# Values of a batch in one tile, keys and queries in one transfer, and tails that leave their list later: attention with two feed-forward layers on one core

## The chip, the cores and the metric

The kernel runs on one NeuronCore of a Trainium2 chip. The metric is the device time of one execution in microseconds (us). Before the change it is 997.43 us, the median of three runs (996.99 to 999.98).

The engines are named as the profile names them: PE is TensorE (matmuls), PEld its weight loads, DVE is VectorE, ACT is ScalarE, POOL is GpSimd, SP is SyncE, whose queue issues nearly all DMAs; a few go out from ACT's queue. PE writes to PSUM, here eight banks of 128 x 512 floats.

## The reference

Four batches, eight heads, 576 positions, head size 64. The attention has a causal mask and a bias from running sums; its output goes through two feed-forward layers.

```python
scores = scale * np.matmul(q, k.transpose(0, 1, 3, 2))
cum = np.cumsum(np.maximum(s, 0.0), axis=-1)
bias = -(cum[:, :, :, None] - cum[:, :, None, :])
scores = np.where(causal, -1000000000.0, scores + np.minimum(bias, 0.0))
attn = softmax(scores)                     # over the keys
x = np.matmul(attn, v)                     # (4, 8, 576, 64), then 2304 tokens x 512
x = ((x @ w_a) * (x @ w_b)) @ w_out        # 512 -> 1536 -> 512
h = x @ w_in                               # 512 -> 2048
out = (np.maximum(h, 0.0) + alpha * np.minimum(h, 0.0)) @ w_out2
```

## The kernel before, in words

**Blocks.** The 2304 tokens are worked off in four feed-forward blocks. Blocks 0, 1 and 2 hold the first 512 positions of batches 0, 1 and 2; block 3 holds those of batch 3 and, besides, the last 64 positions of all four batches, 768 tokens in all. Only block 3 uses a scheme with fewer products (`ffn_seven`). A feed-forward product is made of three matmuls, high part by high part, low by high and high by low (`mm3`, lines 1199 to 1201; the last layer's are lines 1847 to 1849); one of them is 128x512. A block has 816 of them.

**Attention.** `first_attention` does batch 0 before any feed-forward. The attention of batch b + 1 runs inside feed-forward block b, as a list of steps (`attention`): `s01` and `s23` make the scores of a pair of heads, `av` (matmuls at line 810, for batch 0 at line 817) multiplies probabilities by values.

**Tails.** The last 64 queries of every head are the tails. There is one unit for each batch and pair of heads, sixteen in all, in a list of their own (`all_tails`) with three steps each: `ready` loads what the unit needs and makes its bias, `s4` (line 750) computes the scores, `av_b` (line 837) multiplies by the values. Between `s4` and `av_b` lies a chain: reductions on DVE, exponentials on ACT, scaling, a transposition on DVE into `zt`, a DMA from `zt` to DRAM (`zd`), and one back into `pb`, of which there is one buffer. The order of units is that of batches 0, 1, 2, 3. `TAILS = 0.7, 2.85` says over which part of the blocks' time the list is spread.

**The planner.** The class `Order` holds a clock of its own (`run.now`) that adds up planned times of PE and of every chain of steps. It decides in which order and on which engine instructions are recorded; on the chip each engine follows its own list strictly, and semaphores do the rest. A step of the tails leaves the list (`tail_due`) when its share of the time is reached and `possible` says that the planner's clock has what the step needs: `seen` asks for data that are there at most 100 ns from now.

**Values.** `load_v(b, hp, u)` loads the values of one pair of heads, once for `av` (u = 0) and once more for the tails (u = 1), into one of four buffers `vb`. For batch 0 and u = 0 that is one DMA. Otherwise it is four DMAs of 64 KB, one for each fourth partition, and for the tails two more of 16 KB after a `memset` on POOL (line 474).

**Keys and queries.** `load_kq(b, hp, 0)` loads a pair's keys and queries for batches 0 and 1 with two DMAs of 256 KB, one for each half of the partitions. In DRAM (`kq_a`) every head has its rows twice.

**DMA issue.** All DMAs of SP and ACT share eight semaphores in rotation (DMAHW0 to 7 in the order below); a DMA waits for the former user of its semaphore to have landed.

Of the kernel before, what the change touches and what calls it, by code (L numbers as in the profile page):

```python
# [65 lines left out]
TAILS = 0.7, 2.85  # L66
# [151 lines left out]
def attention_two_moe_kernel(  # L218
# [37 lines left out]
    W32, RAW, KQ, VB, CB, KL, TOPS = 4, 5, 3, 4, 3, 2, 2  # L256
# [4 lines left out]
    of_raw, of_kq, of_w32, of_w, of_vb, of_t, of_pb, of_c0, of_c1, of_kl = (  # L261
        Slots(n) for n in (RAW, KQ, W32, 6, VB, 4, 1, CB, 2, 0)
# [195 lines left out]
    def load_v(b, hp, u):  # L458
        c0 = 2 * hp * D
        got = []  # L460

        def chain():
            yield of_vb
            vr = raw.tile([P, 5, 2 * D], F32, name="vb", tag="vb", bufs=VB)
            got.append(vr)
            if b + u < TURN:
                yield from dma(
                    vr[:, 0:4, :], v[b, 0:QA, c0:c0 + 2 * D].rearrange("(c p) d -> p c d", p=P)
                )
                return  # L470
            keys = v[b, 0:QA, c0:c0 + 2 * D].rearrange("(c j k) d -> j k c d", j=4, k=32)
            if u:
                yield {"pool": 240}, SEEN
                nc.gpsimd.memset(vr[:, 4, :], 0.0)
            for j in range(4):
                yield from dma(vr[j::4, 0:4, :], keys[j])
                if u and j < 2:
                    k0 = QA + 32 * j
                    yield from dma(vr[j::4, 4, :], v[b, k0:k0 + 32, c0:c0 + 2 * D])

        v_t[b, hp, u] = got, run.spawn(chain(), slack=SL_QK)
# [44 lines left out]
    def load_sums(b, h, u):  # L526

        got = []

        def chain():  # L530
            yield of_c1 if u else of_c0
            nk = S if u else QA
            cb = raw.tile([P, nk], F32, name=f"cb{u}", tag=f"cb{u}", bufs=2 if u else CB)
# [260 lines left out]

    def av(b, hp):
# [6 lines left out]
        got, ready = v_t.pop((b, hp, 0))  # L802
        run.need(ready)
        at = slot()
        pv = banks[at]
        for r in range(4 if turned else 0):
            for c in range(r + 1):
                for j in range(2):
                    p = pts[(2 * hp + j) % 4].rearrange("p (i t n) -> p i t n", i=4, n=32)
                    nc.tensor.matmul(  # L810
                        pv[64 * j:64 * j + 64, r * P:(r + 1) * P],
                        got[0][:, c, j * D:(j + 1) * D], p[:, :, r * (r + 1) // 2 + c, :],
                        start=c == 0, stop=c == r,
                    )
        for c in range(0 if turned else 4):
            for j in range(2):
                nc.tensor.matmul(
                    pv[64 * j:64 * j + 64, c * P:QA], got[0][:, c, j * D:(j + 1) * D],
# [3 lines left out]
        run.give(of_vb)  # L822
# [3 lines left out]
    def av_b(b, hp):  # L826

        settle((b, hp, 4))
        got, ready = v_t.pop((b, hp, 1))
        run.need(ready)  # L830
# [3 lines left out]
        for c in range(5):  # L834
            for j in range(2):
                p = pb.rearrange("p (i t n) -> p i t n", i=4, n=32)
                nc.tensor.matmul(  # L837
                    pv[64 * j:64 * j + 64], got[0][:, c, j * D:(j + 1) * D],
# [3 lines left out]
        run.give(of_vb)  # L842
# [6 lines left out]
    def first_attention():  # L849
# [16 lines left out]
        for i in range(HP):  # L866
            load_v(0, i, 0)
# [48 lines left out]
    def attention(a):  # L916
# [7 lines left out]
        def loads(i):  # L924
            load_kq(a, i, 0)
            if a >= SUMS_PE:
                for j in range(2):
                    load_sums(a, 2 * i + j, 0)
            load_v(a, i, 0)
# [16 lines left out]
    def all_tails():  # L946

        def ready(b, i):
            load_kq(b, i, 1)
            load_sums(b, i, 1)  # L950
            load_v(b, i, 1)
            biases(b, i, (4,))

        units = [(b, i) for b in range(B) for i in range(HP)]
# [254 lines left out]
    def seen(*chains):  # L1209
        return all(c.done and c.time <= run.now + 100 for c in chains)  # L1210

    def possible(f, args):
# [6 lines left out]
        if f == av:  # L1219
            keys = [(b, 2 * hp + k, r) for k in range(2) for r in (0, 2, 3)]  # L1220
            return all(k in e_t and seen(e_t[k]) for k in keys) and seen(v_t[b, hp, 0][1])
# [728 lines left out]
```

## Time and profile before

| | us |
|---|---|
| runs without a profile, median (range) | 997.43 (996.99 to 999.98) |
| the profiled execution | 1002.63 |
| its span on the core | 1000.8 |
| PE busy in the span | 971.4 |
| DVE, ACT, POOL busy | 752.6, 551.9, 222.4 |

The profiled execution is longer than its span by what lies ahead of the first instruction and behind the last. PE is the engine that is nearly always busy. A share of busy time over the whole span hides where it pauses, so the stretches of the blocks and the pauses themselves are shown further down. A time in brackets behind an instruction is the idle time of its engine just before it, with what ended it; "issue" there means that the profile shows nothing that the engine waited for. PEclk is the clock that the chip granted to PE, as a share of 2.4 GHz.

### The profile page before, as it was taken

What the parts mean: (1) busy time and instruction counts of PE and PEld (TensorE: products, weight loads), DVE (VectorE), ACT (ScalarE), POOL (GpSimd) and SP (SyncE); (2) the same over time, 40 slices, a digit from 0 to 9 for tenths busy, and PEclk for the clock granted to TensorE, in tenths of its full rate; (3) what the DMA queues carried; (4) which work ended last, traced back from release to release, by engine and by line L of the source; (5) the groups of instructions that cost most, each with busy time, mean ns of one, the idle gap of its engine ahead of it and who ended that gap; (6) DMA issues with size and microseconds to landing.
All of it is one profiled execution on the core that took longest, in us unless ns stands there. A gap on an engine that the chain in (4) does not pass through costs nothing.

```text
span 1000.8 us, 15919 instructions
## 1 busy us (share of the span) xinstructions
PE 971.4 (97%) x5267; PEld 815.3 (81%) x5267; DVE 752.6 (75%) x1735; ACT 551.9 (55%) x1156; POOL 222.4 (22%) x287
## 2 busy tenths in 40 slices
PE   7999999999979997999999999999999999999997
PEld 6677877788868875778888887888899999999996
DVE  8897779868767874978568577877587888787782
ACT  7866666667554534665356354554463334476453
POOL 3131111112243342543124444342000000000000
PEclk9999999999998998999999999999999999999999
DMA  9599987799787888589578849666213222112202
GB/s 261 156 317 357 334 287 263 280 323 326 256 262 234 261 239 265 157 272 300 179 240 245 269 136 278 207 183 215 84 43 100 70 84 75 53 49 79 64 1 63
DMA packets 140115, 196.78 MB, mean 197 GB/s; under 512 B 35776, under 2 KB 79808, under 8 KB 140032
## 3 DMA queue, kind: packets, MB, share of 16 engines
q1 hardware_dynamic: 130240, 177.93, 56.8%
q10 hardware_dynamic: 9792, 17.83, 4.7%
q8 instruction: 41, 0.67, 0.3%
q14 instruction: 42, 0.34, 0.1%
HBM read 152.13 MB, written 43.59 MB: 196 GB/s over the span
## 4 chain that ended last, share of the span: by engine, by line
PE 83%; DVE 7%; DMA 6%; issue 2%; ACT 1%; SPq 0%; POOL 0%; ACTq 0%; DVEq 0%; POOLq 0%
PE bank L1199 19%; PE bank L1200 18%; PE bank L1201 18%; PE bank L1847 4%; PE bank L1849 4%; PE bank L1848 4%; PE bank L810 3%; PE bank L1700 2%; PE bank L1699 2%; PE bank L1701 2%; DMA zd<-zt 2%; DVE z L298 2%; PE bank L552 1%; PE bank L750 1%; PE bank L837 1%
## 5 line engine op out<-in xcount | busy, mean ns | idle before, releaser
L1199 PE MATMUL bank<-xh,wh 128*128 128x512 f32 (+1 forms) x620 | 239.7, 387 | 1.9 <-DVE g L298 1.9
L1200 PE MATMUL bank<-xl,wh 128*128 128x512 f32 (+1 forms) x620 | 235.0, 379 | 1.1 <-DVE xl L298 1.1
L1201 PE MATMUL bank<-xh,wl 128*128 128x512 f32 (+1 forms) x620 | 234.6, 378 | 0.0
L290 ACT ACTIVATE wh<-raw 128x512 fp32r<-128x512 f32 (+1 forms) x198 | 116.0, 594 | 155.0 <-PE bank L1200 74.6
L1199 PEld LDWEIGHTS bank<-xh,wh 128*128 128x128 f32 x620 | 116.7, 188 | 26.0 <-issue 3.2
L1200 PEld LDWEIGHTS bank<-xl,wh 128*128 128x128 f32 x620 | 116.9, 188 | 20.0 <-DVE xl L298 1.8
L1201 PEld LDWEIGHTS bank<-xh,wl 128*128 128x128 f32 x620 | 116.8, 188 | 19.5
L307 DVE TENSOR_TENSOR wl<-raw,wh 128x512 fp32r<-128x512 f32 (+1 forms) x140 | 88.5, 646 | 46.8 <-ACT wh L290 46.0
L307 POOL TENSOR_TENSOR wl<-raw,wh 128x512 fp32r<-128x512 f32 x64 | 85.8, 1342 | 105.3 <-ACT wh L290 69.2
L282 ACT ACTIVATE z<-z,mn 128x512 f32<-128x512 f32 (+4 forms) x144 | 82.7, 577 | 18.6 <-DVE mn L298 18.0
L1199 PE MATMUL bank<-gh,wh 128*128 128x512 f32 (+1 forms) x240 | 91.4, 381 | 1.6 <-ACT gh L290 1.6
L1200 PE MATMUL bank<-gl,wh 128*128 128x512 f32 (+1 forms) x240 | 90.0, 375 | 0.2 <-DVE gl L307 0.2
L1201 PE MATMUL bank<-gh,wl 128*128 128x512 f32 (+1 forms) x240 | 89.6, 373 | 0.0
L980 ACT ACTIVATE top<-raw 128x512 f16<-128x512 bf16 x90 | 69.2, 783 | 17.5 <-DMA raw<-in_w_dram 16.7
L1847 PE MATMUL bank<-wh,gh 128*128 128x512 f32 x192 | 76.5, 399 | 0.0
L1849 PE MATMUL bank<-wh,gl 128*128 128x512 f32 x192 | 74.9, 390 | 0.0
L1848 PE MATMUL bank<-wl,gh 128*128 128x512 f32 x192 | 74.8, 390 | 0.0
L290 ACT ACTIVATE gh<-g 128x512 fp32r<-128x512 f32 x84 | 52.4, 624 | 36.6 <-DVE g L298 35.4
L307 DVE TENSOR_TENSOR gl<-g,gh 128x512 fp32r<-128x512 f32 x70 | 55.6, 794 | 19.0 <-ACT gh L290 18.0
L625 POOL TENSOR_SCALAR_AFFINE_SELECT z<-z 64x64 f32<-64x64 f32 (+2 forms) x80 | 35.7, 452 | 112.2 <-DVE z L615 63.8
L290 ACT ACTIVATE wh<-w 128x512 fp32r<-128x512 f32 x66 | 40.9, 626 | 29.7 <-PE bank L1200 10.4
L298 DVE STREAM_TRANSPOSE zt<-z 128x384 f32<-128x384 f32 (+2 forms) x88 | 55.5, 647 | 2.1 <-DMA zd<-zt 1.1
(152 smaller groups left out, 1923.0 us busy)
## 6 DMA issues: line engine op xcount, KB each, us to landing
raw<-w_d SPq DMA_DIRECT2D x91, 512.0 KB, 4.7
raw<-in_w_dram SPq DMA_DIRECT2D x90, 512.0 KB, 5.8
w_d<-w ACTq DMA_DIRECT2D x46, 256.0 KB, 5.6
zd<-zt SPq DMA_DIRECT2D x48, 192.0 KB, 4.2
pt<-zd SPq DMA_DIRECT2D x48, 192.0 KB, 4.2
kq<-in_kq_a_dram SPq DMA_DIRECT2D x16, 512.0 KB, 6.8
vb<-in_v_dram SPq DMA_DIRECT2D x112, 64.0 KB, 4.7
zd<-zt SPq DMA_DIRECT2D x24, 256.0 KB, 2.6
```

The source lines that it names most:

```text
L282: nc.scalar.activation(o, i, func, **k)
L290: nc.scalar.activation(o, i, AF.Copy, scale=by)
L298: f(*args, **k)
L307: (nc.gpsimd if eng == "pool" else nc.vector).tensor_tensor(o, i0, i1, op=ALU.subtract)
L625: nc.gpsimd.affine_select(d, d, pattern=pattern, base=0, channel_multiplier=1, compare_op=ALU.is_ge, fill=MASKED,)
L980: nc.scalar.activation(top.bitcast(F16).rearrange("p (n t) -> p n t", t=2)[:, :, 1], r.bitcast(BF16)[:, 4:4 + 4 * WN].rearrange("p (n t) - ...
L1199: nc.tensor.matmul(o, wh, ih, start=first, stop=False)
L1200: nc.tensor.matmul(o, wh, il, start=False, stop=False)
L1201: nc.tensor.matmul(o, wl, ih, start=False, stop=last)
L1847: nc.tensor.matmul(acc[t], gh[:, c], wh, start=first, stop=False)
L1848: nc.tensor.matmul(acc[t], gh[:, c], wl, start=False, stop=False)
L1849: nc.tensor.matmul(acc[t], gl[:, c], wh, start=False, stop=last)
```

## The change

Four things. The values of a batch go into one tile `v_sb` for all pairs and for the tails, loaded at once: one DMA for batch 0, for each other batch four of 256 KB and two of 64 KB. There is one such tile; `v_uses` counts its readers, and the next batch's load is planned when the last reader has run. The tails of batch 0 alone (third in the new order) have a small tile `vt` of their own, one buffer, six DMAs a unit. A pair's keys and queries come in one DMA of 128 partitions. The tails' list begins at 0.45 instead of 0.7 and goes through the batches as 1, 2, 0, 3. And a step of the list leaves only when its data have been there for a while by the planner's clock: 3 us for `s4`, 7 us for `av_b`. The buffers of the tails' bias sums (`cb1`) go from two to one.

```diff
-TAILS = 0.7, 2.85
+TAILS = 0.45, 2.75
+TAIL_ORDER = 1, 2, 0, 3
+SURE = {"s4": 3000.0, "av_b": 7000.0}
...
+    v_sb = raw.tile([P, 5, DM], F32, name="v_sb")
+    nc.gpsimd.memset(v_sb[:, 4, :], 0.0)
+    v_uses = {b: 2 * H // 2 if b else H // 2 for b in range(B)}
+    def load_v(b):
+        def chain():
+            yield of_v
+            if not b:
+                yield from dma(v_sb[:, 0:4, :], v[b, 0:QA, :].rearrange("(c p) d -> p c d", p=P))
+                return
+            keys = keys_of(b, slice(0, DM))
+            for i in range(0, 4, 2):
+                yield from dmas(*((v_sb[j::4, 0:4, :], keys[j]) for j in range(i, i + 2)))
+            yield from dmas(
+                *((v_sb[j::4, 4, :], v[b, QA + 32 * j:QA + 32 * j + 32, :]) for j in range(2))
+            )
+        v_t[b] = run.spawn(chain(), slack=SL_QK)
+    def v_used(b):
+        v_uses[b] -= 1
+        if not v_uses[b]:
+            run.give(of_v)
...
             else:
-                own = [slice(j * D, (j + 1) * D) for j in range(2)]
-                yield from dmas(*((kq[o], kq_a[b, 2 * hp + j, o]) for j, o in enumerate(own)))
+                r0 = 2 * hp * P + D
+                yield from dma(kq, kq_a[b].rearrange("h p n -> (h p) n")[r0:r0 + P])
...
     def av(b, hp):
...
-        got, ready = v_t.pop((b, hp, 0))
-        run.need(ready)
+        while not v_t[b].done and any(args[0] == b - 1 for _, args in tails):
+            tail()
+        run.need(v_t[b])
...
     def av_b(b, hp):
         settle((b, hp, 4))
-        got, ready = v_t.pop((b, hp, 1))
-        run.need(ready)
+        own = v_t[b, hp] if b == TAIL_ORDER[2] else None
+        run.need(own[1] if own else v_t[b])
...
-        units = [(b, i) for b in range(B) for i in range(HP)]
+        units = [(b, i) for b in TAIL_ORDER for i in range(HP)]
...
-    def seen(*chains):
-        return all(c.done and c.time <= run.now + 100 for c in chains)
+    def seen(*chains, margin=-100.0):
+        return all(c.done and c.time + margin <= run.now for c in chains)
...
-            return (b, hp, 4) in e_t and seen(e_t[b, hp, 4], v_t[b, hp, 1][1])
+            return (b, hp, 4) in e_t and seen(
+                e_t[b, hp, 4], v_t[b, hp][1] if (b, hp) in v_t else v_t[b], margin=SURE["av_b"]
+            )
         if f == s4:
-            return seen(kq_t[b, hp, 1][1], z_t[b, hp, 4][1])
+            return seen(kq_t[b, hp, 1][1], z_t[b, hp, 4][1], margin=SURE["s4"])
```

What it does to the order of instructions is shown at three places. In the rows, `kq` with 704 columns belongs to a tail's `ready`, `zd<-zt` with 640 columns is a tail's store, `pb<-zd` its load back, `raw` a weight, `cb` a bias sum. First SP, before, from the store of tail unit (1, 1) to its load back; the waits stand in brackets:

```order
L323 DMA zd<-zt 128x640 [waits DMAHW5_49,DVE_49]
L323 DMA pt_114<-zd 128x4x96 [waits DMAHW7_49]
L323 DMA kq<-in_kq_b_dram 128x704 [waits PE_49]
L323 DMA cb_4348<-cum_d 64x576 [waits DMAHW0_49]
L323 DMA raw<-w_d 128x2x512 [waits DMAHW1_49,Activation_49,Pool_49]
L323 DMA vb<-in_v_dram 32x4x128 [waits DMAHW3_49]
L323 DMA vb<-in_v_dram 32x4x128 [waits DMAHW4_49]
L323 DMA pb<-zd 128x4x160 [waits DMAHW5_49]
```

and now, for the unit (2, 1), which comes at about the same place in the list:

```order
L327 DMA zd<-zt 128x640 [waits DMAHW4_49,DVE_49]
L327 DMA zd<-zt 128x384 [waits DMAHW5_49,DVE_49]
L327 DMA cb_3852<-cum_d 128x512 [waits DMAHW7_49,DVE_49]
L327 DMA zd<-zt 128x384 [waits DMAHW0_49,DVE_49]
L327 DMA raw<-w_d 128x2x512 [waits DMAHW1_49,Pool_49]
L327 DMA cb_3808<-cum_d 64x576 [waits DMAHW2_49]
L327 DMA pb<-zd 128x4x160 [waits DMAHW4_49,DMAHW3_49]
```

The V loads have gone from between the two. Over all sixteen units one to three V loads stood there in fifteen before; now eleven have none and five have two.

Second PE, before, at the start of block 0's second feed-forward layer, where `xh` and `xl` are the first layer's output:

```order
L1200 MATMUL bank_106<-gl,wh 128x512
L1201 MATMUL bank_106<-gh,wl 128x512
L1199 MATMUL bank_101<-xh_107,wh 128x512
L1200 MATMUL bank_101<-xl_108,wh 128x512
L1201 MATMUL bank_101<-xh_107,wl 128x512
L1199 MATMUL bank_101<-xh_107,wh 128x512
```

and now:

```order
L1237 MATMUL bank_106<-gl,wh 128x512
L1238 MATMUL bank_106<-gh,wl 128x512
L1236 MATMUL bank_101<-xh_107,wh 128x512
L1237 MATMUL bank_101<-xl_108,wh 128x512
L1238 MATMUL bank_101<-xh_107,wl 128x512
L777 MATMUL bank_99<-kq 128x288
L777 MATMUL bank_100<-kq 128x288
L1236 MATMUL bank_101<-xh_107,wh 128x512
```

An `s4`, that of unit (1, 0), has come in behind the first three matmuls. From it on 99 feed-forward matmuls stand ahead of its `av_b`. Over the list these distances were 75 to 108, on average 87; now they are 96 to 132, on average 110.

Third DVE at the same place, before, from the last `xl` to the first input `m` of the second layer's `g`:

```order
L298 SCALAR_TENSOR_TENSOR xl_108<-bank_106,xh_107 128x512
L298 TENSOR_SCALAR sm<-sm 128x1 x3
L298 RECIPROCAL sm<-sm 128x2
L298 TENSOR_SCALAR sm<-sm 128x1
L317 TENSOR_SCALAR z<-z,sm 128x128
L298 RECIPROCAL sm<-sm 128x2
L317 TENSOR_SCALAR z<-z,sm 128x256
L317 TENSOR_SCALAR z<-z,sm 128x128
L298 STREAM_TRANSPOSE zt<-z 128x384
L317 TENSOR_SCALAR z<-z,sm 128x256
L317 TENSOR_SCALAR m<-m,alpha_sb 128x512
```

and now:

```order
L302 SCALAR_TENSOR_TENSOR xl_108<-bank_106,xh_107 128x512
L302 ISA z,mn<-bank_99,z 128x288
L302 ISA mn 128x1
L302 TENSOR_SCALAR sm<-sm 128x1 x2
L302 ISA z,mn<-bank_100,z 128x288
L302 ISA mn 128x1
L302 TENSOR_SCALAR sm<-sm 128x1 x2
L302 RECIPROCAL sm<-sm 128x2 x2
L302 TENSOR_TENSOR mn<-mn 128x1
L321 TENSOR_SCALAR z<-z,sm 128x128 x2
L321 TENSOR_SCALAR z<-z,sm 128x256 x2
L321 TENSOR_SCALAR m<-m,alpha_sb 128x512
```

The two reductions of 288 columns and the minimum of the tail stand ahead of `m` now; one transposition has moved behind it.

## Rows read from the trace of the kernel before

**Rows 1.** The page: the span, and each engine's busy time, share and instructions.

```profile
span 1000.8 us, 15919 instructions
PE 971.4 (97%) x5267; PEld 815.3 (81%) x5267; DVE 752.6 (75%) x1735; ACT 551.9 (55%) x1156; POOL 222.4 (22%) x287
```

**Rows 2.** Stretches of blocks 0, 1, 2: length, busy times (instructions), clock, DMA share, GB/s.

```profile
48.67:261.60 212.93, 211.00 (x1079) 168.09 (x1078) 173.16 (x370) 143.42 (x272) 42.50 (x47) 1.00 0.89 302
261.60:507.00 245.40, 229.64 (x1234) 186.01 (x1233) 176.77 (x410) 128.54 (x268) 90.17 (x116) 0.97 0.79 242
507.00:726.00 219.00, 218.28 (x1204) 179.34 (x1203) 154.25 (x375) 109.81 (x238) 77.48 (x98) 1.00 0.67 210
```

**Rows 3.** Waits of PE: who for whom, us in total, times, longest.

```profile
PE bank L837 <- DMA zd<-zt: 6.4, 2, 4.2
PE bank L837 <- issue: 5.3, 2, 5.1
```

**Rows 4.** PE in order of time: start, length, instruction [idle before]; s4 L750, av_b L837.

```profile
273.69 1.13 PE L750 MATMUL bank<-kq 128*128 128x288 f32 x4
...
299.35 1.34 PE L837 MATMUL bank<-pb,vb 128*64 128x64 f32 x20 [5.14 <-issue]
...
364.62 1.13 PE L750 MATMUL bank<-kq 128*128 128x288 f32 x4
...
393.50 1.34 PE L837 MATMUL bank<-pb,vb 128*64 128x64 f32 x20 [4.16 <-DMA zd<-zt]
...
405.41 1.13 PE L750 MATMUL bank<-kq 128*128 128x288 f32 x4
...
431.15 0.39 PE L1199 MATMUL bank<-xh,wh 128*128 128x512 f32 x1
431.38 0.39 PE L1200 MATMUL bank<-xl,wh 128*128 128x512 f32 x1
...
434.27 0.80 PE L837 MATMUL bank<-pb,vb 128*64 128x64 f32 x20 [2.28 <-DMA zd<-zt]
```

**Rows 5.** Stretches, columns as in rows 2: the three in which the clock stood lower.

```profile
298.52:305.35 6.83, 6.00 (x31) 4.90 (x32) 3.26 (x5) 1.60 (x5) 1.39 (x1) 0.50 0.37 121
390.68:397.51 6.83, 4.00 (x27) 3.34 (x28) 0.00 (x0) 0.82 (x2) 0.00 (x0) 0.50 0.93 261
435.05:438.46 3.41, 3.41 (x9) 2.73 (x9) 2.97 (x6) 2.00 (x4) 0.00 (x0) 0.50 0.85 254
```

**Rows 6.** PE in order of time: three other pauses.

```profile
168.88 0.50 PE L1199 MATMUL bank<-xh,wh 128*128 128x512 f32 x1 [1.93 <-DVE g L298]
...
387.89 0.50 PE L1199 MATMUL bank<-gh,wh 128*128 128x512 f32 x1 [1.55 <-ACT gh L290]
...
399.74 0.50 PE L1200 MATMUL bank<-xl,wh 128*128 128x512 f32 x1 [1.15 <-DVE xl L298]
```

**Rows 7.** The queues of ACT and SP in order of time, from 382 us.

```profile
382.11 0.40 ACTq L1136 DMA_DIRECT2D w_d<-raw  x1
...
382.68 6.77 SPq L323 DMA_DIRECT2D vb<-in_v_dram  x2
389.49 0.59 SPq L323 DMA_DIRECT2D pb<-zd  x1
```

**Rows 8.** Waits of SP's queue, columns as in rows 3.

```profile
SPq L323 <- DMA w_d<-raw: 34.3, 11, 8.4
```

**Rows 9.** The tile vb: its DMAs, ns on SP's queue min/median/max, and their landing.

```profile
L323 SPq DMA_DIRECT2D vb<-in_v_dram x148: 367/611/1662, 7.7 to 684.0; - x148
...
DMA to landing us min/median/max: 1.9/4.7/10.7
```

**Rows 10.** One stretch, columns as in rows 2: batch 0's last av to batch 1's first.

```profile
46.60:85.40 38.80, 38.80 (x182) 30.16 (x180) 34.20 (x92) 27.05 (x59) 10.49 (x10) 1.00 0.99 312
```

**Rows 11.** DVE's groups by form: busy us, mean ns | idle before.

```profile
L298 DVE CUSTOM_DVE_ANT_0 z<-bank,z 128x288 f32<-128x288 f32 x32 | 14.4, 450 | 6.7 <-PE bank L750 6.2
...
L298 DVE TENSOR_TENSOR mn<-mn 128x1 f32<-128x1 f32 x16 | 4.9, 309 | 0.3
```

More of the change, by code (lines that the diff above doesn't have):

```diff
@@ L255, in attention_two_moe_kernel @@
     ps = ctx.enter_context(tc.tile_pool(name="ps", bufs=1, space=PSUM))
[L256 removed]
+    W32, RAW, KQ, CB, KL, TOPS = 4, 5, 3, 3, 2, 2
     ZT = 3
@@ L260, in attention_two_moe_kernel @@
     of_early = {0: Slots(3), 2: Slots(3), 3: Slots(4)}
-    of_raw, of_kq, of_w32, of_w, of_vb, of_t, of_pb, of_c0, of_c1, of_kl = (
-        Slots(n) for n in (RAW, KQ, W32, 6, VB, 4, 1, CB, 2, 0)
+    of_raw, of_kq, of_w32, of_w, of_v, of_vt, of_t, of_pb, of_c0, of_c1, of_kl = (
+        Slots(n) for n in (RAW, KQ, W32, 6, 1, 1, 4, 1, CB, 1, 0)
     )
@@ L460, in load_v, with load_vt @@
+    def load_vt(b, hp):
+        own = slice(2 * hp * D, 2 * hp * D + 2 * D)
         got = []
         def chain():
[L463 to L481, printed above, removed]
+            yield of_vt
+            vt = raw.tile([P, 5, 2 * D], F32, name="vt")
@@ new lines, in chain @@
+            got.append(vt)
+            keys = keys_of(b, own)
+            yield {"pool": 240}, SEEN
+            nc.gpsimd.memset(vt[:, 4, :], 0.0)
+            for i in range(0, 4, 2):
+                yield from dmas(*((vt[j::4, 0:4, :], keys[j]) for j in range(i, i + 2)))
+            yield from dmas(
+                *((vt[j::4, 4, :], v[b, QA + 32 * j:QA + 32 * j + 32, own]) for j in range(2))
+            )
+        v_t[b, hp] = got, run.spawn(chain(), slack=SL_QK)
+    def v_used(b):
+        v_uses[b] -= 1
+        if not v_uses[b]:
+            run.give(of_v)
@@ L532, in chain @@
             nk = S if u else QA
-            cb = raw.tile([P, nk], F32, name=f"cb{u}", tag=f"cb{u}", bufs=2 if u else CB)
+            cb = raw.tile([P, nk], F32, name=f"cb{u}", tag=f"cb{u}", bufs=1 if u else CB)
             got.append(cb)
@@ L793, in settle, with v_of @@
             run.need(e_t.pop(key))
+    def v_of(b, hp, c, j):
+        o = (2 * hp + j) * D
+        return v_sb[:, c, o:o + D]
     def av(b, hp):
@@ L821, in av @@
         run.pe(4 * 1280 / 2.4)
-        run.give(of_vb)
+        v_used(b)
         parts = (x[b % 2][:, hp, :] for x in (xh, xl))
@@ L837, in av_b @@
                 nc.tensor.matmul(
-                    pv[64 * j:64 * j + 64], got[0][:, c, j * D:(j + 1) * D],
+                    pv[64 * j:64 * j + 64],
+                    own[0][0][:, c, j * D:(j + 1) * D] if own else v_of(b, hp, c, j),
                     p[:, 2 * j:2 * j + 2, c, :], start=c == 0, stop=c == 4,
@@ L841, in av_b @@
         run.pe(5 * 107)
-        run.give(of_vb)
+        if own:
+            run.give(of_vt)
+        else:
+            v_used(b)
         run.give(of_pb)
@@ L865, in first_attention @@
             load_kq(0, i, 0)
-        for i in range(HP):
-            load_v(0, i, 0)
+        load_v(0)
         run.pump()
@@ L928, in loads @@
                     load_sums(a, 2 * i + j, 0)
-            load_v(a, i, 0)
+            if not i:
+                load_v(a)
         lead = [(loads, (0,)), (both, (a, 0, (0, 1)))]
@@ L950, in ready @@
             load_sums(b, i, 1)
-            load_v(b, i, 1)
+            if b == TAIL_ORDER[2]:
+                load_vt(b, i)
             biases(b, i, (4,))
-        units = [(b, i) for b in range(B) for i in range(HP)]
+        units = [(b, i) for b in TAIL_ORDER for i in range(HP)]
         steps = [(ready, units[0])]
@@ L1220, in possible @@
             keys = [(b, 2 * hp + k, r) for k in range(2) for r in (0, 2, 3)]
-            return all(k in e_t and seen(e_t[k]) for k in keys) and seen(v_t[b, hp, 0][1])
+            return all(k in e_t and seen(e_t[k]) for k in keys) and seen(v_t[b])
         if f == av_b:
-            return (b, hp, 4) in e_t and seen(e_t[b, hp, 4], v_t[b, hp, 1][1])
+            return (b, hp, 4) in e_t and seen(
+                e_t[b, hp, 4], v_t[b, hp][1] if (b, hp) in v_t else v_t[b], margin=SURE["av_b"]
+            )
         if f == s4:
-            return seen(kq_t[b, hp, 1][1], z_t[b, hp, 4][1])
+            return seen(kq_t[b, hp, 1][1], z_t[b, hp, 4][1], margin=SURE["s4"])
         r = args[2] if f == s23 else 0
```

8 lines of the change are left out of this document (4 added, 4 removed).

## The prediction

> **What bounds the kernel now.** I read the engines' shares first, then the stretches of the three feed-forward blocks that run beside attention, then who TensorE (PE) waited for, and last the instructions at those waits.
>
> PE is busy 971.4 of the span's 1000.8 us; no other engine comes near [rows 1]. So the time is PE's work plus PE's pauses plus what a low clock stretches. The change leaves PE's work alone: the two programs hold the same matmuls, shape by shape, in another order. What it can move is the pauses. They lie unevenly: the first of the three stretches (block 0) has PE busy 211.00 of 212.93 us, the third 218.28 of 219.00, but the second (block 1) 229.64 of 245.40, with a mean granted clock of 0.97 [rows 2].
>
> The waits of PE name the place: the matmuls of line 837, which is av_b (the tails' probabilities times values), waited 6.4 us for a DMA and 5.3 us under "issue" [rows 3]. Three pauses make nearly all of that: 5.14 us at 299.35, 4.16 at 393.50 and 2.28 at 434.27 [rows 4], 11.58 us together. Behind each of the three the clock stands at 0.50 (1.2 GHz): over 6.83, 6.83 and 3.41 us, in which PE was busy 6.00, 4.00 and 3.41 us [rows 5]. At half clock half of that is lost: 3.00 + 2.00 + 1.70 = 6.70 us. The lesser pauses of 1.93, 1.55 and 1.15 us in the feed-forward itself [rows 6] were followed by no such stretch.
>
> Why does av_b wait? Its probabilities go from s4 (line 750) through the softmax, a transpose on VectorE (DVE), a store to DRAM and a load back (pb). From the end of s4's matmuls to av_b this took 299.35 - (273.69 + 1.13) = 24.5 us, 393.50 - (364.62 + 1.13) = 27.8 us and 434.27 - (405.41 + 1.13) = 27.7 us [rows 4]; in all three av_b started as soon as it could. Between s4 and av_b the list had put only 78, 78 and 102 feed-forward matmuls. One takes 0.23 us (431.15 to 431.38 [rows 4]), so that is 18, 18 and 23 us of cover, plus the attention's matmuls in between. Part of the chain's length is the queue of SyncE (SP). Eight semaphores go round among the transfers, and each transfer on SP first waits until the one that had its semaphore before, some eight transfers back, has landed (the order shows these waits as DMAHW0 to 7). So a small transfer costs a place as a large one does. At 382.68 a pair of V loads holds SP for 6.77 us: the second has the semaphore of a weight store that ScalarE (ACT) issued at 382.11. The pb load stands behind it and goes out at 389.49, 24 us after its s4 [rows 7]. Stores of this kind alone held SP for 34.3 us in 11 waits, 8.4 the longest [rows 8].
>
> **The change part by part.** *The list leaves later.* av_b now goes only when the planner's clock is 7 us past the data, s4 when it is 3 us past. Counted in the new program, 96 to 132 feed-forward matmuls stand between s4 and av_b, on average 110 where it was 87; 23 more are 5.2 us. With the attention's matmuls between, counted at their columns, the gap is 26 to 36 us of PE work; before it was 19 to 30. If every chain took 27.8 us, the longest above, the sixteen gaps would lack 3.2 us in all; if none did, nothing. I take 0.8 us, since eleven of the sixteen chains have no V load between the tails' store and pb any more; before, fifteen had one to three. So the three pauses give 11.58 - 0.8 = 10.8 us.
>
> *The clock.* If the pauses go, the low stretches behind them go: 6.7 us. It stays at nothing gained if pauses of that kind turn up elsewhere; the lesser ones above cost no clock. I take all of it.
>
> *V in one tile.* 148 V transfers had a median of 611 ns each on SP's queue and 4.7 us from issue to landing [rows 9]: 90 us of SP, and 148 x 4.7 / 8 = 87 us in which, put together, all eight semaphores were theirs. The new program has 43: one for batch 0, six for each other batch, six for each of the four pairs whose tails have an own tile. 105 fewer free 64 us of SP and 62 of the semaphores. SP bounds nothing by itself; what it gives is a shorter chain, already counted. Twelve of sixteen memsets leave POOL (one is added at the start): nothing on the path.
>
> *Its price in block 0.* Batch 1's V, 1.18 MB, now comes in one lump behind av(0, 3) instead of pair by pair. At the 302 GB/s of that stretch [rows 2] it is 3.9 us of all DMA engines, in a place where their share is 0.99 [rows 10]. The weight loads behind it come that much later once, and no more: the bytes were to be moved in that block anyway. I take 0 and keep 3.9 us for the range.
>
> *Keys and queries.* Eight transfers of 512 KB replace sixteen of 256 KB, with the same bytes; eight issues fewer on SP. Nothing on the path.
>
> *Tails sooner, batch 1 first.* Two more units of s4 and two more of av_b move into block 0, where DVE is busy 173.16 of 212.93 us [rows 2]. The one place where this meets a pause is the start of the second feed-forward, 168.88, where PE waited 1.93 us for DVE's g [rows 6]. There the new order puts an s4 on PE (1.13 us [rows 4]) and ahead of g on DVE its two reductions and one minimum, 2 x 0.45 + 0.31 = 1.2 us [rows 11]. If both pushes fall together the pause grows by 0.1 us; if PE stands waiting anyway, by 1.2 us. I take 0.6. The rest of the two units lies in DVE's 39.8 free us there.
>
> *Sum.* -10.8 - 6.7 + 0.6 = -16.9 us. Made against the profiled execution of 1002.63 us (span 1000.8) that is 985.7; the runs without a profile have a median of 997.43, 5.2 us lower, so the forecast there is 997.43 - 16.9 = 980.5 us. Whether those runs pause as long at av_b I can't see; their spread of 3 us (996.99 to 999.98) says that something of that size varies.
>
> **The rivals.** *Half of it comes back in block 0.* DVE there is 81% busy and the DMA engines 0.89 [rows 2]; the two units that move in could pause PE as the three did before, each at a mean of (11.58 + 6.70) / 3 = 6.1 us. One such pause gives 986.6 us, two give 992.7. For it: block 0 is the fullest of the three. Against: it has one pause of 1.93 us so far, and the new gaps there are 99 to 120 matmuls.
>
> *The change doesn't do what it says.* The margin is on the planner's clock, not on the chip's. If the chain stretches as the list does (the 102 matmuls at 405.41 were not enough, and some new gaps are no longer), the pauses stay: 997.4 us. Against: the chains that waited had V loads before them in SP's queue.
>
> *One V tile makes av wait; slower.* The single tile can be filled anew only when its last reader is through: batch 1's V after av(0, 3), 38.8 us before av(1, 0) in the old trace [rows 10]; batch 2's after the last av_b of batch 1, 186 feed-forward matmuls or 42.2 us before av(2, 0); batch 3's has 330, or 75 us. The six transfers go as three pairs among others on SP. If each pair stood 6.77 us, as the one above did, and the last took the longest landing, 10.7 us [rows 9], V would be there in 31.0 us: in time. From 12.8 us a pair on, batches 1 and 2 would be late by 6 x 12.8 + 21.4 - 38.8 - 42.2 = 17 us, all that is won. At 14 us a pair it is 24.4 - 16.9 = 7.5 us slower: 1005 us. The Trainium skill, page "Trainium Kernel Development and Optimization", section "Best Practices", asks for double-buffering so that DMA overlaps compute, and by it this rival would be the outcome. The covers above are longer than the loads, so here I give the rule little weight.
>
> **How the numbers follow.** Forecast, 0.65: 975 to 987 us around 980.5. Half comes back, 0.15: 987 to 993. No effect, 0.11: within 0.3% of 997.4 (994.4 to 1000.4), which is about what a measurement of this kernel can tell from no change. Slower, 0.09: around 1005. So faster by over 0.3%: 0.65 + 0.15 = 0.80; same 0.11; slower 0.09. The low end takes the best of each unknown: 1.4 us more (no residual, no growth in block 0), the 1.55 and 1.15 us in the feed-forward [rows 6], 1.93 at 168.88 and a little more: 973. The high end takes in two pauses in block 0: 993. The 3.9 us of V's lump lies inside it.
>
> **What would show it.** Right: line 869, the new av_b, has pauses below 2 us in sum; block 1's PE share is like block 2's; no stretch at 0.50 between 50 and 700 us; a V load lands well ahead of its first av; the pause at the start of block 0's second feed-forward is 1.9 to 3.2 us. Wrong: pauses at the feed-forward's lines in block 0 that DVE or a weight load ends, a pause at line 842 that a V load ends, or av_b pauses with the V transfers gone, which would put the chain's length elsewhere. What I trust least is that the clock's share comes back whole.

## The result and the profile after

The new kernel takes **984.21 us** (median of 4 runs, 979.92 to 984.49); the kernel before, measured beside it, 998.7 us (996.99 to 1002.35). The ratio is 0.9837, with a 95% interval from 0.9802 to 0.9872: about 14.5 us faster. Three of its four runs lie at 984 us and one at 979.92. The forecast was 980.5 us in a range of 973 to 993. The profiled execution took 983.97 us with a span of 982.2, against 1002.63 and 1000.8.

The page of the new kernel: span, and each engine's busy time, as in [rows 1].

```profile
span 982.2 us, 15766 instructions
PE 966.5 (98%) x5267; PEld 811.9 (83%) x5267; DVE 748.8 (76%) x1719; ACT 560.4 (57%) x1168; POOL 230.4 (23%) x280
```

The stretches of blocks 0, 1 and 2, with the columns of [rows 2], and the one stretch at 0.50 between 50 and 700 us, as in [rows 5]. The blocks are cut at the same feed-forward matmuls as before.

```profile
49.48:266.96 217.48, 215.15 (x1126) 170.65 (x1125) 173.14 (x382) 147.47 (x279) 54.39 (x56) 1.00 0.89 305
266.96:491.11 224.15, 221.59 (x1209) 181.14 (x1208) 175.45 (x401) 126.81 (x263) 86.06 (x105) 0.99 0.80 258
491.11:707.80 216.69, 216.69 (x1181) 178.18 (x1180) 151.85 (x356) 116.20 (x247) 77.62 (x93) 1.00 0.63 197
350.82:354.23 3.41, 2.96 (x7) 2.29 (x8) 3.41 (x10) 0.92 (x2) 0.00 (x0) 0.50 0.54 163
```

Block 1 shrank from 245.40 to 224.15 us, partly because two tails' units now run in block 0, which grew from 212.93 to 217.48. PE pauses 2.56 us in block 1, where it paused 15.76 before.

The longest waits of PE that are not at the very start, as in [rows 3]:

```profile
PE bank L777 <- DVE ovl L311: 3.6, 2, 2.6
...
PE bank L1236 <- DVE sm L302: 1.3, 1, 1.3
```

Line 869 (av_b, which was line 837) has gone from the list: no av_b pauses for its data any more. In its place stands line 777, s4. PE in order of time, with all three pauses of 0.1 us or more between 50 and 700 us, and one av_b that starts without any:

```profile
170.09 0.50 PE L1236 MATMUL bank<-xh,wh 128*128 128x512 f32 x1 [1.32 <-DVE sm L302]
...
227.74 0.75 PE L777 MATMUL bank<-kq 128*128 128x288 f32 x2 [1.01 <-DVE ovl L311]
...
351.27 1.33 PE L777 MATMUL bank<-kq 128*128 128x288 f32 x2 [2.56 <-DVE ovl L311]
...
380.19 0.80 PE L869 MATMUL bank<-pb,v_sb 128*64 128x64 f32 x20
```

The wait of 2.56 us is not for data but for a bank: the second half of s4 writes where the av_b before it had left its result, and DVE had not yet read that. DVE in order of time shows why:

```profile
347.92 1.35 DVE L311 TENSOR_TENSOR qs<-kq,qs 64x512 fp32r<-64x512 f32 x1
349.31 1.77 DVE L321 TENSOR_SCALAR z<-z,sm 128x512 f32<-128x512 f32 x2
351.00 0.21 DVE L311 TENSOR_TENSOR ovl<-bank,ovh 128x64 fp32r<-128x64 f32 x1
```

The reader, `ovl`, takes 0.21 us but stands behind 3.1 us of other attention work in DVE's queue (347.92 to 351.00).

**An account that closes.** Take each kernel's span, subtract PE's pauses of 0.1 us or more, and subtract half of PE's busy time in each stretch at 0.50. What is left is 968.6 us for the kernel before and 968.7 for the new one; over all fourteen kernels of this study it lies between 967.1 and 969.4. So, to within those 2.3 us, the differences here are pauses and clock. Between 48 and 726 us the kernel before had 18.42 us of pauses and lost 6.71 to the clock, 25.1 together; the new one has 4.90 and 1.48 (half of 2.96), 6.4 together. The difference, 18.7 us, is that of the profiled executions (1002.63 - 983.97).

### The profile page after: what moved, and what is told of

It reads as the page before. It is cut to its first block, busy times and chain, and to the rows that moved or that the text cites. A ratio compares the mean times of both kernels' runs of the same rounds, so it can differ in the third digit from the quotient of the medians.

```text
span 982.2 us, 15766 instructions
## 1 busy us (share of the span) xinstructions
PE 966.5 (98%) x5267; PEld 811.9 (83%) x5267; DVE 748.8 (76%) x1719; ACT 560.4 (57%) x1168; POOL 230.4 (23%) x280
## 4 chain that ended last, share of the span: by engine, by line
PE 92%; DVE 3%; DMA 2%; ACT 1%; issue 1%; ACTq 0%; POOL 0%; SPq 0%; POOLq 0%; DVEq 0%
PE bank L1236 21%; PE bank L1237 20%; PE bank L1238 20%; PE bank L1886 4%; PE bank L1888 4%; PE bank L1887 4%; PE bank L842 3%; PE bank L1739 2%; PE bank L1738 2%; PE bank L1740 2%; PE bank L579 2%; PE bank L777 1%; DVE z L302 1%; PE bank L598 1%; PE bank L869 1%; PE bank L804 1%
## 5 line engine op out<-in xcount | busy, mean ns | idle before, releaser
L1237 PEld LDWEIGHTS bank<-xl,wh 128*128 128x128 f32 x620 | 116.4, 188 | 18.3
L286 ACT ACTIVATE z<-z,mn 128x128 f32<-128x128 f32 (+4 forms) x144 | 82.7, 576 | 19.0 <-DVE mn L302 18.8
L1017 ACT ACTIVATE top<-raw 128x512 f16<-128x512 bf16 x90 | 69.0, 784 | 14.5 <-DMA raw<-in_w_dram 13.3
L311 POOL TENSOR_TENSOR wl<-w,wh 128x512 fp32r<-128x512 f32 x26 | 34.3, 1319 | 109.1 <-ACT wh L294 83.8
L321 DVE TENSOR_SCALAR z<-z,sm 128x512 f32<-128x512 f32 (+4 forms) x100 | 56.8, 594 | 1.1
```

The source lines that it names most:

```text
L286: nc.scalar.activation(o, i, func, **k)
L311: (nc.gpsimd if eng == "pool" else nc.vector).tensor_tensor(o, i0, i1, op=ALU.subtract)
L321: (nc.gpsimd if eng == "pool" else nc.vector).tensor_scalar(o, i, s0, s1, op0=ALU.mult, op1=ALU.mult)
L1017: nc.scalar.activation(top.bitcast(F16).rearrange("p (n t) -> p n t", t=2)[:, :, 1], r.bitcast(BF16)[:, 4:4 + 4 * WN].rearrange("p (n t) - ...
L1237: nc.tensor.matmul(o, wh, il, start=False, stop=False)
```

## Experiments

Each was timed beside the kernel before on the same chip; the ratio is to that kernel. e2 to e9 ran on one chip and e10 to e13 on another, where the kernel before took about as long (997.68 us, against 997.46 and 999.4). "Pauses + clock" is the account above, between 48 and 726 us of the profiled execution; its second number is the part that the clock cost. It is of one execution; those of e3 and e9 (989.7 and 986.29 us) are the upper ends of their ranges. "Late" gives the margins of s4 / av_b in us. The tails go through the batches as 1, 2, 0, 3 in all kernels with the tile and in e3, e4 and e11, and as 0, 1, 2, 3 in the others.

| kernel | V | spread | late | median us (range) | ratio [95%] | pauses + clock |
|---|---|---|---|---|---|---|
| before | small | 0.70-2.85 | - | 997.5 to 999.4 in four comparisons | 1 | 18.4 + 6.7 |
| new kernel | tile | 0.45-2.75 | 3 / 7 | 984.21 (979.92-984.49) | 0.9837 [0.9802, 0.9872] | 4.9 + 1.5 |
| e2 | tile | 0.45-2.75 | - | 987.0 (985.6-988.9) | 0.9884 [0.9854, 0.9914] | 8.1 + 2.6 |
| e3 | small | 0.45-2.75 | - | 985.56 (982.67-989.7) | 0.9872 [0.9833, 0.991] | 8.6 + 4.2 |
| e4 | small | 0.45-2.75 | 3 / 7 | 983.65 (981.89-983.93) | 0.9844 [0.981, 0.9878] | 4.1 + 1.7 |
| e5 | tile | 0.45-2.75 | 3 / 7, bank 1 | 980.36 (979.45-980.74) | 0.9815 [0.9787, 0.9843] | 3.1 + 0 |
| e6 | small | 0.70-2.95 | - | 987.95 (987.0-989.22) | 0.9888 [0.9859, 0.9916] | 7.2 + 1.7 |
| e7 | small | 0.45-2.60 | - | 987.89 (983.87-989.69) | 0.9877 [0.9843, 0.9911] | 9.5 + 0 |
| e8 | small | 0.58-2.80 | - | 987.29 (984.9-987.5) | 0.9871 [0.9846, 0.9897] | 6.9 + 3.4 |
| e9 | small | 0.70-2.85 | 1 / 4 | 984.97 (983.67-986.29) | 0.9854 [0.9827, 0.988] | 5.6 + 3.2 |
| e10 | tile | 0.70-2.85 | - | 982.63 (982.32-985.04) | 0.985 [0.9832, 0.9869] | 5.2 + 0 |
| e11 | small | 0.45-2.75 | 3 / 7, bank 1 | 985.6 (984.46-985.86) | 0.9873 [0.9855, 0.989] | 3.9 + 1.6 |
| e12 | small | 0.70-2.85 | three av_b: 5 | 984.79 (983.38-986.27) | 0.9867 [0.9848, 0.9886] | 4.3 + 1.7 |
| e13 | small | 0.70-2.85 | 1 / 4, bank 1 | 990.66 (986.48-992.4) | 0.9921 [0.9896, 0.9945] | 7.5 + 3.2 |

My theory going in was the prediction's: the list leaves too soon, and its lateness takes the three pauses and their clock. The rivals: the new spread does it, the V tile does it, or the old list was an unlucky draw.

**e2, the new kernel without the late leaving.**

```diff
-SURE = {"s4": 3000.0, "av_b": 7000.0}
+SURE = {"s4": -100.0, "av_b": -100.0}
```

> The changed kernel with both margins set back to 100 ns ahead, as before: values in one tile, one transfer for keys and queries, the new spread and order of the tails stay. Theory 1 (the distance in the list cures the pauses): the gaps between s4 and av_b fall back to 18 to 25 us of planned time, pauses at av_b return; gain against before 3 to 7 us of the 16, so 991 to 996 us. Theory 2 (the V loads had stretched the chain through the eight semaphores): the chain is short by itself, hardly a pause returns, 982 to 985 us.

Measured: 987.0 us. PE in order of time, its longest pause, and the stretch at 0.50 around it:

```profile
315.29 1.34 PE L869 MATMUL bank<-pb,v_sb 128*64 128x64 f32 x20 [5.09 <-DVE mn L302]
```

```profile
313.67:320.50 6.83, 5.21 (x29) 4.30 (x30) 4.95 (x21) 4.45 (x14) 5.16 (x6) 0.50 1.04 351
```

Only 1.2 us of waiting for pb is left in this kernel. The long pause is av_b's, but DVE ends it with `mn`, a reduction of the scores in the bank that av_b is to overwrite. So without any lateness the three old pauses were gone, which lateness was to have removed. The time lies between the ranges of the two theories: hardly a wait for pb returned, as theory 2 had it, but a wait for a bank came.

**e3, the new spread and batch order alone.**

```diff
-TAILS = 0.7, 2.85
+TAILS = 0.45, 2.75
-        units = [(b, i) for b in range(B) for i in range(HP)]
+        units = [(b, i) for b in (1, 2, 0, 3) for i in range(HP)]
```

> The kernel before with the new spread (0.45 to 2.75) and batch order of the tails alone; small V loads, two transfers for keys and queries, no margins. Theory 1: pauses at av_b as before, 994 to 1001 us. Theory 2: the same, since the V loads are still in the queue. If moving the tails to other places were what helped, it would come down to about 985 us.

Measured: 985.56 us, 11.9 below the kernel before. The theories had 994 to 1001 us; the third case, that other places help, came. PE's two longest waits outside the start are bank waits again:

```profile
PE bank L837 <- DVE mn L298: 4.1, 1, 4.1
...
PE bank L750 <- DVE ovl L307: 1.9, 1, 1.9
```

**e4, late leaving, new spread and order, with the small V tiles and two transfers for keys and queries.**

```diff
+SURE = {"s4": 3000.0, "av_b": 7000.0}
...
+    def seen(*chains, margin=-100.0):
+        return all(c.done and c.time + margin <= run.now for c in chains)
...
```

> The kernel before with the margins (3 and 7 us) and the new spread and order, but with the small V loads and the two transfers for keys and queries. Theory 1: the list's distance alone does it, av_b pauses sum below 3 us, 982 to 987 us. Theory 2: chains of up to 28 us against gaps of 25 to 32 us leave pauses of 1 to 3 us at some units and the low clock behind them, 990 to 997 us.

Measured: 983.65 us, as the new kernel. Of this 2 x 2 (late or not, tile or small V, all at the new spread), the kernels with the V tile are 1.4 and 0.6 us slower, and lateness is worth 1.9 and 2.8 us. Only the 2.8 (e2 against the new kernel) is clear of the scatter; e3's four runs alone spread over 7 us. So I turned to the spread, and to the bank.

**e5, the new kernel with a margin for s4's bank.** s4 leaves only when the readers of its banks are 1 us past on the planner's clock.

```diff
+BANK = 1000.0
-        if not seen(*(reader[i] for i in ring[:rings] if i in reader)):
+        if not seen(
+            *(reader[i] for i in ring[:rings] if i in reader), margin=BANK if f == s4 else -100.0
+        ):
```

> The changed kernel with one more margin: s4 leaves the list only when the banks that it writes have been read for 1 us by the planner's clock. If the pauses of 2.56 and 1.01 us at s4 in the changed kernel, and the 3.4 us at half clock behind the first, come from leaving as soon as the planner sees the bank free, they go and the time is 978 to 981 us. If a pause only moves to the next instruction, it stays at 982 to 986 us. The planned end is 1.0 us later, which both include.

Measured: 980.36 us, the fastest of all, though one of the new kernel's four runs (979.92) was as fast. s4 has gone from PE's waits, and PE has one stretch of 545 us (165 to 710 us) at full clock with 3.1 us of pauses:

```profile
165.00:710.00 545.00, 541.88 (x2962) 443.78 (x2961) 413.91 (x931) 312.14 (x632) 193.31 (x229) 1.00 0.74 238
```

**e6, e7, e8: the kernel before with other spreads.** One line each; the three tell apart a sooner start, a slower pace, and chance.

```diff
-TAILS = 0.7, 2.85
+TAILS = 0.7, 2.95      # e6
+TAILS = 0.45, 2.60     # e7
+TAILS = 0.58, 2.80     # e8
```

> The kernel before with one number changed: the tails' steps begin at 0.70 of block 0 as before, but run to 2.95 instead of 2.85 blocks, so a unit comes every 0.141 block instead of 0.134 (the new kernel has 0.144). Theory 'sooner' (the new spread helps because it begins at 0.45, which takes steps out of block 1): the start is the old one, so 995 to 999 us. Theory 'pace' (it helps because each unit gets more feed-forward matmuls): most of the 12 us come, 985 to 989. Theory 'placement' (where each step falls against its chain is chance, and the old spread was an unlucky draw): anything from 982 to 1000, with no order between this run and the next two.

> The kernel before with the steps begun at 0.45 and ended at 2.60: the new start with the old pace (0.134 block for a unit). Theory 'sooner': 985 to 989 us. Theory 'pace': 995 to 999. Theory 'placement': anything from 982 to 1000. The planner's own end of this list lies 3 us later, so 3 us may come on top in each case.

> The kernel before with 0.58 and 2.80: half of the new start, pace 0.139 (half of the new pace). Theories 'sooner' and 'pace' both: between, 990 to 993 us. Theory 'placement': no reason for the middle; below 988 or above 995 speaks for it.

Measured: 987.95, 987.89, 987.29 us. A sooner start without the pace and the pace without a sooner start gave the same, and half of both gave no less. Neither theory survives as the only cause. With e3, which also has the new batch order, that is four other spreads with the same rule and the same small V tiles, all 11 to 12 us faster than the old one. What is left is "placement": the old list is an unlucky draw. That is argued from five lists and not shown; that a sooner start and a slower pace are each enough alone isn't excluded, nor was the batch order tried by itself.

**e9, the late leaving alone, at the old spread.**

```diff
+SURE = {"s4": 1000.0, "av_b": 4000.0}
...
```

`seen` and `possible` take the margins as in the change.

> The kernel before with the late leaving alone, at the old spread and with the small V tiles: s4 goes 1 us and av_b 4 us after their data on the planner's clock (with the new kernel's 3 and 7 us the last unit doesn't fit before the old end). The prediction's own reading (the list leaves too soon, and its lateness is what takes the three pauses): the pauses of av_b that a DMA ends sum to under 3 us, and the time is 983 to 988 us. Rival (the spread does it, lateness gives 2 to 3 us): av_b still pauses for pb by 8 us or more, and the time is 993 to 997.

Measured: 984.97 us, 14.4 below the kernel before. PE's waits hold no av_b at all; the longest is at a feed-forward matmul:

```profile
PE bank L1201 <- DVE sm L300: 2.8, 1, 2.8
...
PE bank L1201 <- DVE g L300: 1.9, 1, 1.9
```

So with lateness alone the three pauses go, as the prediction had it, but not by the way that it gave, more matmuls to cover the chain. The trace tells for each of the three units the PE work between s4's end and av_b (the cover) and the time from s4's end until pb has landed (the chain), in us:

| unit | before: cover, chain | e9 | e12 (below) | new kernel |
|---|---|---|---|---|
| (0, 2) | 19.4, 24.3 | 21.6, 17.7 | 24.1, 23.8 | 26.8, 18.3 |
| (1, 1) | 21.8, 27.4 | 21.0, 15.9 | 23.0, 18.3 | 28.7, 21.0 |
| (1, 2) | 25.3, 27.6 | 25.3, 19.4 | 30.7, 24.4 | 25.7, 17.2 |

In e9 the cover of these three grew by 2.2 us at most; their chains shrank by 6.6 to 11.5 us. The rows of (1, 1) in e9, PE's s4, SP's load back and PE's av_b:

```profile
375.22 1.13 PE L752 MATMUL bank<-kq 128*128 128x288 f32 x4
...
389.08 0.38 SPq L325 DMA_DIRECT2D pb<-zd  x1
...
400.35 0.80 PE L839 MATMUL bank<-pb,vb 128*64 128x64 f32 x20
```

Over all sixteen units lateness did add cover: 95 feed-forward matmuls on average between s4 and av_b in this trace, against 86 before. It was not needed for taking the pauses in e3, where another spread and batch order did it.

**e10, the V tile at the old spread, without lateness.** The batch order stays the new one, which the single tile needs; the single transfer of keys and queries and the one buffer of `cb1` stay too.

```diff
-TAILS = 0.45, 2.75
+TAILS = 0.7, 2.85
-SURE = {"s4": 3000.0, "av_b": 7000.0}
+SURE = {"s4": -100.0, "av_b": -100.0}
```

> The new kernel with both margins taken back and the steps at the old spread, 0.70 to 2.85, so that of its edits the V tile, the single transfer of keys and queries and the batch order are left. The list has the old spread's pattern, batch 1 first; the V loads stand elsewhere in SP's queue, and there are 105 fewer. Theory 'V loads' (the prediction's: the V transfers ahead of pb lengthen the chains, and the old list's three pauses are theirs): the three pauses go, 985 to 988 us. Rival 'bare list' (a list without margin at this spread comes close to its chains whatever the V loads do): av_b pauses for pb at about 270 to 400 us by 5 us or more, 991 to 999 us.

Measured: 982.63 us, 15.1 below the kernel before. av_b still waits for pb, three times, 1.92 us the longest, with no stretch at 0.50:

```profile
PE bank L869 <- DMA pb<-zd: 3.7, 3, 1.9
```

That is less than the bare list's 5 us in its expectation, and better than the V theory's 985. But the chains from s4's end to pb's landing did not become much shorter: 18.7 us on average over the sixteen units and 26.0 at most, against 19.7 and 27.6 before. The V loads lie elsewhere, the batches come in another order, and so every step has moved; e10 can't say which of these did it.

**e12, the kernel before with only the three pausing units held back.** This asks whether the three pauses are the whole story.

```diff
+HELD = {(0, 2): 5000.0, (1, 1): 5000.0, (1, 2): 5000.0}
...
-            return (b, hp, 4) in e_t and seen(e_t[b, hp, 4], v_t[b, hp, 1][1])
+            return (b, hp, 4) in e_t and seen(
+                e_t[b, hp, 4], v_t[b, hp, 1][1], margin=HELD.get((b, hp), -100.0)
+            )
```

> The kernel before with one edit: av_b of the three units that paused, (0, 2), (1, 1) and (1, 2), goes 5 us after its data on the planner's clock; all other steps keep their rule. The list is the old one up to 270 us and from 500 us on. Theory 'the three pauses' (they and the half clock behind them are the whole difference): 983 to 988 us, with no pause of those three units. Rival 'they come back' (the list between is shifted, and other units, above all (1, 0), whose gap shrinks from 28 to 20 us on the planner's clock, wait in their place): 990 to 996.

Measured: 984.79 us. The av_b of the three units, in PE's order of time; compare [rows 4], where they stand at 299.35, 393.50 and 434.27 with 5.14, 4.16 and 2.28 us ahead of them:

```profile
301.76 0.80 PE L839 MATMUL bank<-pb,vb 128*64 128x64 f32 x20
...
383.88 0.80 PE L839 MATMUL bank<-pb,vb 128*64 128x64 f32 x20
...
422.99 0.80 PE L839 MATMUL bank<-pb,vb 128*64 128x64 f32 x20
```

No pause, and none came in their place beyond 1.2 us; one stretch of 3.41 us at 0.50 came behind the old pause of 1.93 us at the start of block 0's second layer. Three steps held back bring 12.9 us, where the whole change brings 14.5. That is the most direct support for the prediction's main reading, that these three pauses and their clock are most of what can be won. For the way that they go it is mixed (table above): at (1, 1) a cover of 23.0 us would not have held the old chain of 27.4; the chain itself fell to 18.3.

**e11 and e13, the bank's margin with small V tiles**: on e4, and on e9.

```diff
+BANK = 1000.0
-        if not seen(*(reader[i] for i in ring[:rings] if i in reader)):
+        if not seen(
+            *(reader[i] for i in ring[:rings] if i in reader), margin=BANK if f == s4 else -100.0
+        ):
```

> The late leaving at the new spread with the small V tiles, plus 1 us of margin on the readers of the bank that s4 is to write (the edit that took the new kernel to 980.4). Theory 'V is neutral': 979.5 to 982 us, as with the one V tile, and no pause of s4. Rival 'the one V tile is worth something once the pauses are gone': 983 or more.

> The kernel before with margins alone, at the old spread: s4 1 us and av_b 4 us after their data, and 1 us on the readers of s4's bank. Theory 'margins do all' (data and bank waits both go, spread and V tile are neutral): 980 to 983 us. Rival 'the new spread adds something of its own': 984 to 986, as with the data margins alone.

Measured: 985.6 and 990.66 us; both theories that I leaned to missed. In e11 the rival's 983 or more came; e13 lies beyond the rival's range too. s4 waits in neither, but a third kind of wait stands in both. e13: PE, then ACT, then SP, each in order of time:

```profile
389.43 0.50 PE L1202 MATMUL bank<-xh,wh 128*128 128x512 f32 x1 [3.26 <-ACT xh L293]
```

```profile
388.16 0.77 ACT L983 ACTIVATE top<-raw 128x512 f16<-128x512 bf16 x1 [5.00 <-DMA raw<-in_w_dram]
388.81 1.06 ACT L293 ACTIVATE xh<-bank 128x512 fp32r<-128x512 f32 x2
```

```profile
381.30 1.27 SPq L326 DMA_DIRECT2D vb<-in_v_dram  x2
382.67 0.54 SPq L326 DMA_DIRECT2D raw<-in_w_dram  x1
383.25 0.43 SPq L326 DMA_DIRECT2D pt<-zd  x1
383.73 0.51 SPq L326 DMA_DIRECT2D cb<-cum_d  x1
384.34 0.53 SPq L326 DMA_DIRECT2D zd<-zt  x1
384.96 0.61 SPq L326 DMA_DIRECT2D vb<-in_v_dram  x1
```

Read from the bottom up: SP works without a break through small transfers, V loads among them; the weight `raw` goes out at 382.67 and lands at 388.08. ACT stands 5.00 us in front of the weight's first step, `top`, with the next `xh` behind it in its queue, though `xh` needs no weight. PE waits 3.26 us for `xh`, and a stretch of 3.41 us at 0.50 follows. That the V loads are what made the weight late is read from the queue and not shown. In e11 the same place shows:

```profile
384.08 0.77 ACT L983 ACTIVATE top<-raw 128x512 f16<-128x512 bf16 x1 [4.21 <-DMA raw<-in_w_dram]
```

and PE waits 2.29 us for `xh`. From 370 to 392 us SP issues 20 to 26 transfers, 6 to 10 of them V, in e6, e9, e11 and e13, and 11 to 18 without any V in the four kernels with the tile (new, e2, e5, e10). From 372 to 400 us a `top` waits over 1 us for its `raw` in seven of the ten kernels with small V (7.27 us in the kernel before; not in e3, e4, e8) and in none of the four with the tile. But that stretch is the favourable one. From 50 to 700 us the waits of `top` for `raw` add up to 5.0 to 11.8 us in the four kernels with the tile and to 6.9 to 17.5 in the ten without, and the new kernel has one of 6.9 us. Its row over the whole span, as in [rows 3]:

```profile
ACT top L1017 <- DMA raw<-in_w_dram: 13.3, 6, 6.9
```

The longest, 6.92 us, ends at 309.44, with a pair of V transfers at 302.82 ahead of the weight on SP (the weight went out at 304.58); PE did not pause there. So whether the tile takes weight waits off the path isn't shown. Nor is that it explains the 5.2 us between e11 and e5: their lists differ too, they ran on two chips, and the account of the profiled runs gives 2.4 of it.

## Why the prediction held, and where it didn't

**What bounds the kernel: right.** The remainder of 967.1 to 969.4 us in fourteen kernels says that little else than pauses and clock moves. The three pauses and the three low stretches were the right place: e12 holds back just the three steps behind them and gives 984.8.

**The list leaves later, -10.8 us: right in size, wrong in being the only way, and only half right in the mechanism.** The 11.58 us are gone in the new kernel, and e9 gives 984.97 with (smaller) margins alone. But e3 does it with the spread and the batch order (985.56) and e10 with the V tile, the batch order and the single transfer of keys and queries (982.63). Apart they bring 11.9, 14.4 and 15.1 us; added up that would be 41, and together they bring 14.5. They remove the same three pauses. The prediction took the chains as given and priced the cover. In the new kernel the cover of the three units did grow, by 0.4 to 7.4 us, but their chains also shrank by 6 to 10 us, which the sum did not have; in e9 it was the chains nearly alone. The prediction read "the list leaves too soon" as a property of the rule; seven lists without any margin (before, e2, e3, e6, e7, e8, e10) show that the old list was the worst of them by about 10 us. At the new spread lateness is worth 2 to 3 us, of which only the pair with the tile is clear of the scatter.

**The clock, -6.7: mostly right.** The three stretches went, and one came: 3.41 us around the new pause of s4. Net 5.2 us. "No stretch at 0.50 between 50 and 700" was wrong by that one.

**Where the time goes next: missed.** The prediction looked for new pauses at the feed-forward's lines in block 0 and at av's V. They came at s4's bank, 2.56 and 1.01 us plus 1.48 of clock: 5.0 us with no term in the sum. Against that, smaller pauses of the kernel before that it had left standing went too, 4.9 us of them (18.42 - 11.58 - 1.93), those at 387.89 and 399.74 in [rows 6] among them. The two about cancel, and that the sum came out so near is luck to that extent. In the profiled executions the terms are -11.58 for the three pauses, -5.23 for the clock, -0.61 at the start of block 0's second layer, +3.57 at s4's bank and -4.91 for the smaller pauses: about -18.7 us, where the forecast had -16.9. The prediction's "half of it comes back" was priced at a mean of 6.1 us a pause; one of 2.56 us with its clock cost 4.0.

**Block 0's second feed-forward, +0.6: wrong sign.** The pause shrank from 1.93 to 1.32 us, below the 1.9 to 3.2 that were named as a sign. It moves with the list (0.57 in e11, 2.07 in e8), and the step took the worse half of a range whose lower end should have lain below nothing.

**V in one tile, 0: near in the 2 x 2, its way not confirmed.** The kernels with the tile are 1.4 and 0.6 us slower at the new spread, inside the scatter. The prediction let the tile act only through a shorter chain to pb. Over all units that chain hardly changed: 19.1 us on average where it was 19.7, 24.7 at most where it was 27.6. Over all kernels it is the same with and without the tile: 18.3 us on average in the four with it, 18.4 in the ten with small V. It is shortest in e5 and e9 (17.2 in both), and in e9 fourteen of the sixteen units have V loads between store and load back. (Counted in the traces, the kernel before also has them in fourteen units, and the new one in four.) So the V loads ahead of pb are not what makes chains long on the whole.

**The slower rival: didn't come.** The last V transfers for batches 1 and 2 went out on SP in these rows, and the first av on PE in the next:

```profile
60.87 0.49 SPq L327 DMA_DIRECT2D v_sb<-in_v_dram  x1
...
302.82 1.66 SPq L327 DMA_DIRECT2D v_sb<-in_v_dram  x2
```

```profile
86.25 0.55 PE L842 MATMUL bank<-pt,v_sb 128*64 128x128 f32 x6
...
332.75 0.44 PE L842 MATMUL bank<-pt,v_sb 128*64 128x128 f32 x4
```

V lands at 62.98 and 306.13, 23 and 27 us ahead. The six transfers took 15.5 and 21.7 us from the first issue to the last landing, well inside the 31.0 that the prediction allowed. The Trainium skill, page "Trainium Kernel Development and Optimization", section "Best Practices", asks for double-buffering; the single tile here cost 1.4 us in the pair e3 and e2 and 0.6 in e4 and the new kernel, both inside the scatter, and e5 with it is the fastest.

**From the profile to the median: 3.7 us off.** The sum was made against an execution of 1002.63 us and taken from the median of 997.43. The profiled executions differ by 18.7 us, the medians by 14.5. The kernel before varies from 996.0 to 1002.9 us over all its runs, and its profiled one was near the upper end, so it had more to lose. The prediction said that it couldn't see this; it could have made the sum smaller by it.

**What stays open.** Why the old list is the worst draw: the chains of its three units were 24.3, 27.4 and 27.6 us long, while e6's for the same units were 22.3, 25.3 and 21.3 with nothing changed but the pace. The trace shows that the three were long in different places. At (1, 1) the transposition into `zt` was done at 373.38, but the store went out only at 379.88, behind a load back (`pt`) that left SP at 379.40, just after a store issued at 372.22 had landed (379.34); then came the 6.77 us of [rows 7]:

```profile
372.55 0.83 DVE L298 STREAM_TRANSPOSE zt<-z 128x640 f32<-128x640 f32 x1
...
379.40 0.38 SPq L323 DMA_DIRECT2D pt<-zd  x1
379.88 0.45 SPq L323 DMA_DIRECT2D zd<-zt  x1
```

At (1, 2) DVE came to the transposition only at 421.23, 14.7 us after s4's end; at (0, 2) the store took 5.7 us to land and the load 7.4. Why just these chains met covers that were too short is what no run here explains, and no run took one of the delays away by itself.

## What to carry to other kernels

When three pauses hold most of what can be won, many edits that move the steps around them win it (here all thirteen changed kernels but e13 won 10 us or more), so a gain says little about the edit: try two or three neutral shifts of the order (here 0.70 to 0.58) before crediting one, and hold back just the pausing steps to see what the pauses are worth. Add up pauses and low-clock stretches for each kernel; if the remainder is constant, there is little else to explain. Look at both sides of a wait, the chain's length and the work that covers it, before saying which of them an edit changed. When the data waits are gone, look at who still has to read the bank, and at what stands in front of that reader in its engine's queue.

## What the runs showed of the hardware

The clock followed pauses of PE unevenly. Those of 4.05 us and longer (e2, e3, before) had a stretch of 6.83 us at 1.2 GHz around them, those from 2.28 to 3.26 us one of 3.41, but for one of 2.41 us in e7, which had none. About 2 us went either way: 1.95 to 2.07 us in e3, e6 and e8 had one of 3.41; 1.93 us at the start of block 0's second feed-forward was followed by no low stretch in the kernel before and in e6, and by 3.41 us of it in e9, e12 and e13. So a pause of 1.93 us cost 1.9 us or, with half of the 3.41 us lost, 3.6.
